# A linear attention and MLP kernel on one core: the second MLP product formed from seven sub-block products, in a new instruction order

## The chip, the cores and the metric

The kernel runs on one core of a Trainium2 chip. A core has TensorE (PE; its weight loads, PEld, overlap its matmuls), VectorE (DVE), ScalarE (ACT), GpSimd (POOL) and SyncE (SP), which only issues DMAs here. Each engine works through its own queue in order; waits between them are semaphores. The metric is the device time of one execution in microseconds, as the median of several runs. Before the change that is 877.42 us (three runs, 877.41 to 877.72).

## The reference

Two kinds of layers alternate, A B A B, over x of 2048 rows by 448 columns; float32 throughout:

```python
def _A_ref(x, wqkv, wo):
    B, S, D = x.shape
    H = 16; Dh = D // H
    ...
    q, k, v = qkv[0], qkv[1], qkv[2]
    phi = lambda t: jnp.where(t > 0, t + 1, jnp.exp(t)) + 1e-6
    pq, pk = phi(q), phi(k)
    kv = jnp.einsum("bhsd,bhse->bhde", pk, v)
    z = jnp.einsum("bhsd->bhd", pk)
    num = jnp.einsum("bhqd,bhde->bhqe", pq, kv)
    den = jnp.einsum("bhqd,bhd->bhq", pq, z)[..., None] + 1e-6
    o = num / den
    return (lambda x, *d: x.transpose(*d))(o, 0, 2, 1, 3).reshape(B, S, D) @ wo

def _B_ref(x, w1, b1, w2, b2):
    h = jnp.einsum("bsd,df->bsf", x, w1) + b1
    h = _gelu(h)
    return jnp.einsum("bsf,fd->bsd", h, w2) + b2

x = A_x
x = x + _A_ref(_layernorm(x, axis=-1), A_wqkv, A_wo)
x = x + _B_ref(_layernorm(x, axis=-1), B_w1, B_b1, B_w2, B_b2)
x = x + _A_ref(_layernorm(x, axis=-1), A_wqkv, A_wo)
x = x + _B_ref(_layernorm(x, axis=-1), B_w1, B_b1, B_w2, B_b2)
```

qkv is x @ wqkv, cut into q, k and v of 16 heads with 28 columns each. LayerNorm has no weights; the MLP's hidden width F is 1792.

## The kernel before, in words

**Tiles and precision.** The 2048 rows are 16 tiles of 128; four tiles are a block. A float32 product is made of fp32r matmuls: each operand is split into a high part (a cast to fp32r) and a low part (the difference), and three products high x high, high x low, low x high are summed in a PSUM bank. The last 64 of 448 columns are handled with both parts in one 128-row piece.

**The order.** `ORDER` (from line 15 on) is one string of tokens for each of the two A-B pairs. `run` goes through it; a token such as `gh13` calls the function `gh` with number 13, `:a`, `:d`, `:p` names an engine (or a buffer), `>` and `<` reach into the other pair. So the tokens' sequence is the order in every engine's queue and in SP's.

**Attention.** `ld` loads a tile of x, `a` takes its mean and variance (`stats`, lines 349 to 356: BN_STATS, BN_AGGREGATE, an addition, all VectorE), `ar` the power -0.5 on GpSimd, `n` the normalization on VectorE (`norm`, line 365). The tile is turned either by TensorE transposes (`T`, `ht`) or by 32x32 transposes on VectorE (`tu`) with a store to DRAM (`st`) and four loads that put the squares in place (`sp`). `xh` and `xl` split it. `K` and `Q` project, `ke` to `kl` and `qe`, `qp` form phi; `qs` stores phi(q) to DRAM. `G` sums x-transposed times phi(k) over all tiles; from it come kv, the mask and one matrix per group (`kv`, `mask`, `m`). Then each tile of phi(q) is loaded (`pl`), divided by its denominator (`pz` on GpSimd, `pd`, `pm` on VectorE), turned (`pT`, or `pu`, `ps`, `pp`), split (`qh`, `ql`), multiplied (`o`, `oc`) and added to x (`oa`).

**MLP.** `la` and `ln` are the LayerNorm again, into a buffer xm; `mT` or `mu`, `ms`, `mp` turn it, `yh` and `yl` split it into a block's XH and XL, of which there are two each (line 382). `lb` adds b2 to x on GpSimd. For each block `f` (lines 884 to 895) forms one of 14 chunks of 128 hidden units by 512 rows: 11 matmuls of 512 columns, into one of two `h` banks; `g` applies bias and gelu on ScalarE (line 900); `gh` casts it on ScalarE, `gl` takes the difference on VectorE (line 910), in rings A and B of two buffers. `y` (or its four parts `u`) adds a chunk to the block's four row tiles, which stay in the four `acc` banks:

```python
pe.matmul(o, gh[:, r], w2h[:, i, s], start=first, stop=False)   # L918
pe.matmul(o, gh[:, r], w2l[:, i, s], start=False, stop=False)   # L919
pe.matmul(o, gl[:, r], w2h[:, i, s], start=False, stop=last)    # L920
```

After the 14th chunk `ya` adds the bank to x (line 937) and `ys` stores the tile. The next block's attention tail (`pl` to `oa`) and LayerNorm run between a block's `f` and `y`.

**Weights.** `bld`, `bhi` and `blo` load and split w1 (n < 16) and w2 (n from 16 on) once, during the first attention; w1h, w1l, w1x, w2h and w2l stay in SBUF for both pairs.

Of the kernel before, what the change touches and what calls it, by code (L numbers as in the profile page):

```python
# [118 lines left out]
def linear_attn_mlp_kernel(  # L119
# [19 lines left out]
    NF = F // 128  # L139
    G = 112  # L140
    NG = D // G
    TL = D - 64
    LAYERS = 2

    consts = ctx.enter_context(tc.tile_pool(name="consts", bufs=1))
# [174 lines left out]
    def bhi(l, n, e):  # L320
        s = T[l, "bg", n]
        eng = ENG[e or "a"]
        if n >= 16:
            copy(eng, w2h[:, n - 16], s)
            return
# [656 lines left out]
```

## Time and profile before

| | |
|---|---|
| median of the runs | 877.42 us |
| profiled execution, span from first to last instruction | 875.6 us |
| instructions | 11616 |
| TensorE busy | 870.3 us |
| VectorE, ScalarE, GpSimd busy | 477.5, 344.2, 208.7 us |
| granted TensorE clock | 1.0 in all slices |
| DMA | 93.71 MB |

The profile is of one execution; its own device time is not listed beside it, its span is 875.6 us. The busy time of an engine is the union of its instructions' durations. Rows by line give a group of instructions: engine, operation, tiles out<-in with their sizes, count, busy us, mean ns of one, and the idle time ahead of them with what ended it. Timeline rows begin with start and duration in us. Rows by window give, for each engine, the busy us and the count.

### The profile page before, as it was taken

Reading aid. Unit: us, or ns where it says so; the run is one execution under the profiler, and the core shown is the slowest. Engines: PE = TensorE matmul, PEld = TensorE weight load, DVE = VectorE, ACT = ScalarE, POOL = GpSimd, SP = SyncE. Lnnn points to the kernel's source line nnn. Section 1 sums busy time; section 2 is a strip of 40 time slices with the busy share of each in tenths; the row PEclk is TensorE's granted clock in tenths of the full one; section 3 lists DMA queues with packets and bytes.
Section 4 is the critical chain, followed back from the end, with each engine's and each line's share of the span. In section 5 each row is a group of like instructions: output and inputs, shape, how many; then the busy total and the mean of one; then the engine's idle time right before and its main releaser. Section 6 shows DMA issues by size and latency. Waiting matters only on the chain.

```text
span 875.6 us, 11616 instructions
## 1 busy us (share of the span) xinstructions
PE 870.3 (99%) x4189; PEld 774.1 (88%) x4189; DVE 477.5 (55%) x974; ACT 344.2 (39%) x610; POOL 208.7 (24%) x247
## 2 busy tenths in 40 slices
PE   9999999999999999999999999999999999999998
PEld 7999998889888888888899999889898888888887
DVE  7887687758543534442379756875735616212112
ACT  6676744323223223322446555341332232223222
POOL 4555552543210020020022325240311110200000
PEclk9999999999999999999999999999999999999999
DMA  7666545543314203220347442363341251021101
GB/s 240 188 179 223 132 137 160 169 149 94 111 57 107 84 17 112 81 75 25 82 149 232 155 117 64 101 203 109 118 107 43 73 130 64 1 73 36 42 1 43
DMA packets 62762, 93.71 MB, mean 107 GB/s; under 512 B 8816, under 2 KB 57968, under 8 KB 62704
## 3 DMA queue, kind: packets, MB, share of 16 engines
q1 hardware_dynamic: 62400, 92.51, 35.1%
q8 instruction: 33, 0.54, 0.3%
q10 hardware_dynamic: 304, 0.46, 0.2%
q14 instruction: 25, 0.20, 0.1%
HBM read 55.65 MB, written 34.08 MB: 102 GB/s over the span
## 4 chain that ended last, share of the span: by engine, by line
PE 90%; issue 3%; DVE 2%; DMA 2%; ACT 1%; POOL 1%; SPq 0%; POOLq 0%; DVEq 0%; ACTq 0%
PE y L919 10%; PE y L918 10%; PE y L920 10%; PE hp L892 9%; PE hp L891 9%; PE hp L893 9%; PE hp L894 3%; PE hp L895 3%; PE psq L547 2%; PE psq L548 2%; PE psq L549 2%; PE op L827 2%; PE op L828 2%; PE op L826 2%; PE psk L547 1%
## 5 line engine op out<-in xcount | busy, mean ns | idle before, releaser
L910 DVE TENSOR_TENSOR gl<-g,gh 128x512 fp32r<-128x512 f32 x112 | 81.3, 729 | 265.1 <-ACT gh L215 265.1
L900 ACT ACTIVATE g<-hp,b1s 128x512 f32<-128x512 f32 x112 | 76.9, 688 | 258.1 <-PE hp L895 236.1
L919 PE MATMUL y<-w2l,gh 128*128 128x448 f32 x448 | 163.7, 365 | 0.0
L918 PE MATMUL y<-w2h,gh 128*128 128x448 f32 x448 | 163.6, 365 | 0.0
L920 PE MATMUL y<-w2h,gl 128*128 128x448 f32 x448 | 163.6, 365 | 0.0
L892 PE MATMUL hp<-XH,w1l 128*128 128x512 f32 x336 | 130.9, 390 | 0.0
L891 PE MATMUL hp<-XH,w1h 128*128 128x512 f32 x336 | 130.8, 389 | 0.0
L893 PE MATMUL hp<-XL,w1h 128*128 128x512 f32 x336 | 130.8, 389 | 0.0
L215 ACT CAST gh<-g 128x512 fp32r<-128x512 f32 x112 | 69.2, 621 | 137.8 <-PE y L919 131.7
L361 POOL TENSOR_TENSOR brs<-bve,mhalf 128x1 f32<-128x1 f32 x64 | 37.3, 586 | 358.7 <-DVE bve L355 325.5
L918 PEld LDWEIGHTS y<-w2h,gh 128*128 128x128 f32 x448 | 84.1, 188 | 7.4
L919 PEld LDWEIGHTS y<-w2l,gh 128*128 128x128 f32 x448 | 84.1, 188 | 7.3
L920 PEld LDWEIGHTS y<-w2h,gl 128*128 128x128 f32 x448 | 84.1, 188 | 6.6
L893 PEld LDWEIGHTS hp<-XL,w1h 128*128 128x128 f32 x336 | 63.1, 188 | 13.2
L891 PEld LDWEIGHTS hp<-XH,w1h 128*128 128x128 f32 x336 | 63.1, 188 | 12.6
L892 PEld LDWEIGHTS hp<-XH,w1l 128*128 128x128 f32 x336 | 63.1, 188 | 12.5
L757 POOL TENSOR_TENSOR pz<-pq,zb 128x448 f32<-128x448 f32 x32 | 37.3, 1170 | 50.0 <-DVE dn L762 37.1
L539 POOL TENSOR_TENSOR xnl<-x,xnh 128x384 fp32r<-128x384 f32 x32 | 32.6, 1017 | 58.4 <-ACT xnh L215 58.3
L351 DVE BATCH_NORM_STATS2 bst<-x 128x6 f32<-128x448 f32 x64 | 39.5, 617 | 7.7 <-DMA x<-in_A_x_dram 4.2
L894 PE MATMUL hp<-XH,w1x 128*128 128x512 f32 x112 | 43.6, 389 | 0.0
L895 PE MATMUL hp<-XL,w1x 128*128 128x512 f32 x112 | 43.6, 389 | 0.0
L855 POOL TENSOR_TENSOR x<-x,b2b 128x448 f32<-128x448 f32 x32 | 39.5, 1246 | 14.9 <-DVE xm L365 14.9
(174 smaller groups left out, 1569.2 us busy)
## 6 DMA issues: line engine op xcount, KB each, us to landing
x<-in_A_x_dram SPq DMA_DIRECT2D x32, 224.0 KB, 3.5
pq_d<-eq SPq DMA_DIRECT2D x32, 224.0 KB, 2.9
pq<-pq_d SPq DMA_DIRECT2D x32, 224.0 KB, 3.4
x<-x_d SPq DMA_DIRECT2D x32, 224.0 KB, 3.3
sq_a<-sq SPq DMA_DIRECT2D x13, 512.0 KB, 3.0
sp<-sq_a SPq DMA_DIRECT2D x52, 128.0 KB, 3.5
sq_q<-sq SPq DMA_DIRECT2D x12, 512.0 KB, 3.6
sp<-sq_q SPq DMA_DIRECT2D x48, 128.0 KB, 3.1
```

What stands on the lines that cost most here:

```text
L215: act.copy(out, src)
L351: dve.bn_stats(st, xs)
L891: pe.matmul(o, w1h[:, c, s], x.moving(x.hi, c), start=(c == 0), stop=False)
L892: pe.matmul(o, w1l[:, c, s], x.moving(x.hi, c), start=False, stop=False)
L893: pe.matmul(o, w1h[:, c, s], x.moving(x.lo, c), start=False, stop=False)
L894: pe.matmul(o, w1x[:, s], x.moving(x.hi, 3), start=False, stop=False)
L895: pe.matmul(o, w1x[:, s], x.moving(x.lo, 3), start=False, stop=True)
L900: act.activation(T[l, "g", n], T[l, "hp", n], AF.Gelu_apprx_tanh, bias=b1s[:, n % NF:n % NF + 1])
L910: dve.tensor_sub(lo, T[l, "g", n], f(hi))
L918: pe.matmul(o, gh[:, r], w2h[:, i, s], start=first, stop=False)
L919: pe.matmul(o, gh[:, r], w2l[:, i, s], start=False, stop=False)
L920: pe.matmul(o, gl[:, r], w2h[:, i, s], start=False, stop=last)
```

## The change

The second MLP product of a block, 512 rows x 1792 times 1792 x 448, is formed by Strassen's scheme: the gelu output is cut into a11, a12 (rows 0 to 255, hidden units 0 to 895 and 896 to 1791) and a21, a22 (rows 256 to 511), w2 likewise, and seven products of sums of them replace eight. 

- w2 is no longer kept in SBUF. `vd`, `va`, `vh`, `vl`, `vs` load its 14 row chunks, form the five sums of quarters, split all seven and store them to DRAM as `w2_d`, high and low part side by side, 448 columns in all. `cw` loads one of the seven (896 x 448 floats, as 7 chunks in 128 partitions) for each product, into a ring of three buffers, Y, which `vd` uses too.
- `g` writes its chunk into a store of 14 chunks: eight in the second pair of XH and XL, six in a new tile g6. The MLP's own input has one XH and XL instead of two.
- `cs` forms the sums of a block in place, on VectorE, one quarter (two chunks, the last one chunk) at a time; `ch` casts a quarter on ScalarE, `cl` takes the difference on VectorE, in rings A and B or E and F.
- `cp` multiplies a quarter: for each chunk and each of two row tiles a matmul of 448 columns (high part with both parts of the weights) and one of 224 (low part with the high part of the weights, added to the right half of the bank). A product fills two of the four `acc` banks.
- `cf` adds both halves of a bank into x, or subtracts them, for each place that the product goes to.
- LayerNorm: `stats` and `norm` can run on ScalarE (a sum by an accumulating pass, a squared pass, then the scaling). 28 of 32 MLP tiles and 14 of 32 attention tiles (`n` only) use that.
- `pz` stays on GpSimd in all its tokens; its default engine is now VectorE.
- Both strings of `ORDER` are new. The first wqkv pieces are all loaded by SP, and the first product is Q of tile 0 instead of K.

```diff
...
-        "gh0 bld21:xn pd5 bhi18 bhi21 gl0 f1 g1 u0 gh1 gl1 u3 u1 pz4 u2 y1 f2 pm5 pd4 f3 g2 gh2 mc g3 blo18 "
...
+        "cw1 cp4 cp5 pp3 qh6 cw2 qs13 ql6 mu4 mu5 cs12 g11 ch7 ms2 oc6 ch6 cl9 cl6 cp6 qh7 oa6 ql7 oc7 cs5 cs9 la6:a "
...
+        "ys14 ch106 ch107:aEF cl106 cl107 cf51 ys15 cp104 cp105 cp106 cp107 ch109:aEF ch108 cl108 cp108 cl109 cp109 "
+        "ch110 ch111:aEF cl110 cp110 cl111 cp111 cf53 cf52 cf54 ys12 cf55 ys13 "
...
     TL = D - 64
+    HD = D // 2
+    KC = NF // 2
     LAYERS = 2
...
-    BUFS = {"H": 9, "S": 5, "e": 3, "xn": 2, "A": 2, "B": 2, "E": 2, "F": 2, "X": 2, "tail": 2, "small": 2}
+    BUFS = {"H": 9, "S": 5, "e": 3, "xn": 2, "A": 2, "B": 2, "E": 2, "F": 2, "X": 2, "tail": 2, "small": 2, "Y": 3}
     BANKS = {"acc": 4, "h": 2, "m": 2}
...
     pq_d = [dram([S, D], F32, f"pq_d{l}") for l in range(LAYERS)]
+    w2_d = dram([7, 128, KC * D], F32, "w2_d")
     x_d = [x0] + [dram([S, D], F32, f"x_d{l}") for l in range(1, LAYERS)] + [y_out]
     make_identity(nc, ident)
+    eps = consts.tile([128, 1], F32, name="eps")
+    pool.memset(eps, 1e-5)
     mhalf = consts.tile([128, 1], F32, name="mhalf")
...
     w1x = wts.tile([128, F], F32R, name="w1x")
-    w2h = wts.tile([128, NF, D], F32R, name="w2h")
-    w2l = wts.tile([128, NF, D], F32R, name="w2l")
+    g6 = wts.tile([128, 6, 512], F32, name="g6")
...
         s = T[l, "bg", n] = ring(tag, 512 if tag == "xn" else D, "stg")[:, :D]
-        if n < 16:
-            load_piece(w1[:, n // 4 * D:(n // 4 + 1) * D], n % 4, s, sp)
-        else:
-            sp.dma_start(s, w2[rows(n - 16), :])
+        load_piece(w1[:, n // 4 * D:(n // 4 + 1) * D], n % 4, s, sp)
         eng = ENG[e or "a"]
-        if n >= 16:
-            copy(eng, w2h[:, n - 16], s)
-            return
         sl, c = slice(n // 4 * D, (n // 4 + 1) * D), n % 4
...
         eng = ENG[e or "p"]
-        if n >= 16:
-            eng.tensor_tensor(w2l[:, n - 16], s, f(w2h[:, n - 16]), op=OP.subtract)
-            return
         sl, c = slice(n // 4 * D, (n // 4 + 1) * D), n % 4
...
-    def stats(xs):
+    M3, M6, M4, M1, M2, M5, M7 = range(7)
+    W2AT = (1, 5, 2, 4, 0, 3, 6)
+    GOES = {M1: ((0, 0, OP.add), (1, 1, OP.add)), M2: ((1, 0, OP.add), (1, 1, OP.subtract)),
+            M3: ((0, 1, OP.add), (1, 1, OP.add)), M4: ((0, 0, OP.add), (1, 0, OP.add)),
+            M5: ((0, 1, OP.add), (0, 0, OP.subtract)), M6: ((1, 1, OP.add),), M7: ((0, 0, OP.add),)}
+    @op
+    def vd(l, i, e):
+        T["w2o", l, i] = o = ring("Y", KC * D, "w2o").rearrange("p (k h n) -> p k h n", k=7, h=2)
+        for r in range(2):
+            sp.dma_start(o[:, 2 * r:2 * r + 2, 1], w2[rows(r * KC + i), :].rearrange("p (h n) -> p h n", h=2))
+    @op
+    def va(l, i, e):
+        o = T["w2o", l, i][:, :, 1]
+        eng = ENG[e or "p"]
+        for to, x, y, how in ((4, 0, 3, OP.add), (5, 0, 1, OP.add), (6, 2, 3, OP.add),
+                              (1, 1, 3, OP.subtract), (2, 2, 0, OP.subtract)):
+            eng.tensor_tensor(o[:, to], o[:, x], o[:, y], op=how)
+    @op
+    def vh(l, i, e):
+        hi, lo = (T["w2o", l, i][:, :, h] for h in range(2))
+        copy(ENG[e or "a"], hi.bitcast(F32R), lo)
+    @op
+    def vl(l, i, e):
+        hi, lo = (T["w2o", l, i][:, :, h] for h in range(2))
+        (ENG[e or "p"]).tensor_tensor(lo.bitcast(F32R), lo, hi, op=OP.subtract)
+    @op
+    def vs(l, i, e):
+        sp.dma_start(w2_d[:, :, i * D:(i + 1) * D].rearrange("k p n -> p k n"),
+                     T["w2o", l, i].rearrange("p k h n -> p k (h n)"))
+    def stats(xs, e, other):
+        ve = small(1, "bve")
+        mv = small(2, "bmv")
+        if e == "a":
+            act.activation(xs, xs, AF.Identity, accum_out=mv[:, 1:2])
+            act.mul(mv[:, 0:1], mv[:, 1:2], -1.0 / D)
+            act.activation(other(), xs, AF.Square, bias=mv[:, 0:1], accum_out=mv[:, 1:2])
+            act.activation(ve, mv[:, 1:2], AF.Identity, bias=eps, scale=1.0 / D)
+            return mv, ve, True
         st = small(6, "bst")
         dve.bn_stats(st, xs)
-        mv = small(2, "bmv")
         dve.bn_aggr(mv, st)
-        ve = small(1, "bve")
         dve.tensor_scalar(ve, mv[:, 1:2], 1e-5, None, op0=OP.add)
-        return mv, ve
+        return mv, ve, False
     def root(key):
-        mv, ve = T[key]
+        mv, ve, neg = T[key]
         rs = small(1, "brs")
         pool.tensor_tensor(rs, ve, mhalf, op=OP.pow)
-        T[key] = mv, rs
-    def norm(out, xs, mv, rs):
-        dve.tensor_scalar(out, xs, mv[:, 0:1], rs, op0=OP.subtract, op1=OP.mult)
+        T[key] = mv, rs, neg
+    def norm(out, xs, mv, rs, neg, e):
+        if e == "a":
+            nb = small(1, "bnb")
+            if not neg:
+                act.mul(mv[:, 0:1], mv[:, 0:1], -1.0)
+            act.activation(nb, mv[:, 0:1], AF.Identity, scale=rs)
+            act.activation(out, xs, AF.Identity, bias=nb, scale=rs)
+        else:
+            dve.tensor_scalar(out, xs, mv[:, 0:1], rs, op0=OP.add if neg else OP.subtract, op1=OP.mult)
     class Block:
-        def __init__(self):
-            self.hi = ring("XH", 2048, "XH", F32R)
-            self.lo = ring("XL", 2048, "XL", F32R)
+        def __init__(self, r):
+            self.hi = ring(f"XH{r}", 2048, "XH", F32R)
+            self.lo = ring(f"XL{r}", 2048, "XL", F32R)
...
-    BUFS["XH"] = BUFS["XL"] = 2
-    def block(*key):
+    def block(kind, l, b):
+        key = (kind, l, b) if kind == "a" else (kind, l)
         if ("blk", key) not in T:
-            T["blk", key] = Block()
+            T["blk", key] = Block(b % 2)
         return T["blk", key]
...
     def a(l, t, e):
-        T["st", l, t] = stats(T["x", l, t])
+        T["st", l, t] = stats(T["x", l, t], e, lambda: ring("e", 512, "sj")[:, :D])
...
         xs = T["xn", l, t] = T["x", l, t]
-        norm(xs, xs, *T["st", l, t])
+        norm(xs, xs, *T["st", l, t], e)
...
     def pz(l, t, e):
-        T["pz", l, t] = ring(e or f"W{4 if t > 3 else 4 + t % 2}", D, "pz")
-        pool.tensor_tensor(T["pz", l, t], T["pq", l, t], T[l, "zb"], op=OP.mult)
+        T["pz", l, t] = ring(f"W{4 if t > 3 else 4 + t % 2}", D, "pz")
+        ENG[e or "d"].tensor_tensor(T["pz", l, t], T["pq", l, t], T[l, "zb"], op=OP.mult)
...
     def la(l, t, e):
-        T["st", l, t] = stats(T["x", l, t])
+        def xm():
+            T["mn", l, t] = ring("xn", 512, f"xm{l}_{t}")
+            return T["mn", l, t][:, :D]
+        T["st", l, t] = stats(T["x", l, t], e, xm)
     def ln(l, t, e):
-        xn = T["mn", l, t] = ring("xn", 512, f"xm{l}_{t}")
-        mv, rs = T["st", l, t]
-        norm(xn[:, :D], T["x", l, t], mv, rs)
+        if ("mn", l, t) not in T:
+            T["mn", l, t] = ring("xn", 512, f"xm{l}_{t}")
+        norm(T["mn", l, t][:, :D], T["x", l, t], *T["st", l, t], e)
     def lx(l, t, e):
-        mv, rs = T["st", l, t]
-        norm(T["mn", l, t][:, D:], T["x", l, t][:, TL:], mv, rs)
+        norm(T["mn", l, t][:, D:], T["x", l, t][:, TL:], *T["st", l, t], e)
...
+    def gstore(l):
+        if (l, "G2") not in T:
+            T[l, "G2"] = [ring(t, 2048, "g2").rearrange("p (c n) -> p c n", c=4) for t in ("XH1", "XL1")]
+        return T[l, "G2"]
+    def gview(l, half, c, k=1):
+        return gstore(l)[half][:, c:c + k] if c < 4 else g6[:, half * 3 + c - 4:half * 3 + c - 4 + k]
     @op
     def g(l, n, e):
-        T[l, "g", n] = ring("e", 512, "g")
-        act.activation(T[l, "g", n], T[l, "hp", n], AF.Gelu_apprx_tanh, bias=b1s[:, n % NF:n % NF + 1])
-    @op
-    def gh(l, n, e):
-        T[l, "gs", n] = ring("A", 512, "gh", F32R), ring("B", 512, "gl", F32R)
-        copy(ENG[e or "a"], T[l, "gs", n][0], T[l, "g", n])
-    @op
-    def gl(l, n, e):
-        hi, lo = T[l, "gs", n]
-        dve.tensor_sub(lo, T[l, "g", n], f(hi))
-    def y_mm(l, n, j, s=slice(0, D), o=None):
-        gh, gl = T[l, "gs", n]
         i = n % NF
-        first, last = i == 0, i == NF - 1
-        r = rows(j)
-        o = T[l, "y", n // NF, j][:, s] if o is None else o
-        pe.matmul(o, gh[:, r], w2h[:, i, s], start=first, stop=False)
-        pe.matmul(o, gh[:, r], w2l[:, i, s], start=False, stop=False)
-        pe.matmul(o, gl[:, r], w2h[:, i, s], start=False, stop=last)
-    @op
-    def y(l, n, e):
-        for j in range(4):
-            u(l, n * 4 + j, e)
-    @op
-    def u(l, n, e):
-        n, j = divmod(n, 4)
-        if n % NF == 0:
-            T[l, "y", n // NF, j] = bank("acc", f"y{j}")[:, :D]
-        y_mm(l, n, j)
-    @op
-    def ya(l, t, e):
-        xs = T["x", l, t]
-        dve.tensor_tensor(xs, T[l, "y", t // 4, t % 4], xs, op=OP.add)
+        act.activation(gview(l, i // KC, i % KC)[:, 0], T[l, "hp", n], AF.Gelu_apprx_tanh, bias=b1s[:, i:i + 1])
+    def quad(l, r, c, q):
+        return gview(l, c, q * 2, min(2, KC - q * 2))[:, :, r * 256:(r + 1) * 256]
+    def sums(l, n):
+        bk, q = divmod(n, 4)
+        return quad(l, *{M3: (0, 0), M4: (1, 1), M2: (1, 0), M5: (0, 1), M1: (0, 0), M6: (1, 0), M7: (1, 1)}[bk % 7], q)
+    @op
+    def cs(l, n, e):
+        s, q = n // 4 % 5, n % 4
+        a11, a12, a21, a22 = quad(l, 0, 0, q), quad(l, 0, 1, q), quad(l, 1, 0, q), quad(l, 1, 1, q)
+        to, x, y, how = ((a21, a21, a11, OP.subtract), (a12, a12, a11, OP.add), (a11, a11, a22, OP.add),
+                         (a21, a21, a11, OP.add), (a22, a12, a11, OP.subtract))[s]
+        ENG[e or "d"].tensor_tensor(to, x, y, op=how)
+    @op
+    def ch(l, n, e):
+        x = sums(l, n)
+        w = x.shape[1]
+        T[l, "chl", n] = [ring(t, 512, nm, F32R)[:, :w * 256].rearrange("p (c n) -> p c n", c=w)
+                          for t, nm in zip(e[1:] or "AB", ("ch", "cl"))]
+        copy(ENG[e[:1] or "a"], T[l, "chl", n][0], x)
+    @op
+    def cl(l, n, e):
+        hi, lo = T[l, "chl", n]
+        ENG[e or "d"].tensor_tensor(lo, sums(l, n), f(hi), op=OP.subtract)
+    @op
+    def cw(l, n, e):
+        T[l, "w2", n] = ring("Y", KC * D, "w2s", F32R).rearrange("p (c n) -> p c n", c=KC)
+        ENG[e or "s"].dma_start(f(T[l, "w2", n].rearrange("p c n -> p (c n)")), w2_d[W2AT[n % 7]])
+    @op
+    def cp(l, n, e):
+        bk, q = divmod(n, 4)
+        hi, lo = T[l, "chl", n]
+        w = T[l, "w2", bk]
+        if q == 0:
+            T[l, "cp", bk] = [bank(e or "acc", f"cp{j}")[:, :D] for j in range(2)]
+        for c in range(hi.shape[1]):
+            i = q * 2 + c
+            for j in range(2):
+                o = T[l, "cp", bk][j]
+                pe.matmul(o, hi[:, c, rows(j)], w[:, i], start=(i == 0), stop=False)
+                pe.matmul(o[:, HD:], lo[:, c, rows(j)], w[:, i, :HD], start=False, stop=(i == KC - 1))
+    @op
+    def cf(l, n, e):
+        bk, j = divmod(n, 2)
+        b, k = divmod(bk, 7)
+        o = T[l, "cp", bk][j]
+        for part in (o[:, :HD], o[:, HD:]):
+            for r, c, how in GOES[k]:
+                xs = T["x", l, 4 * b + 2 * r + j][:, c * HD:(c + 1) * HD]
+                dve.tensor_tensor(xs, xs, part, op=how)
```

More of the change, by code (lines that the diff above doesn't have):

```diff
@@ L902, in gh @@
-    @op
-    def gh(l, n, e):
-        T[l, "gs", n] = ring("A", 512, "gh", F32R), ring("B", 512, "gl", F32R)
-        copy(ENG[e or "a"], T[l, "gs", n][0], T[l, "g", n])
-    @op
-    def gl(l, n, e):
-        hi, lo = T[l, "gs", n]
-        dve.tensor_sub(lo, T[l, "g", n], f(hi))
-    def y_mm(l, n, j, s=slice(0, D), o=None):
-        gh, gl = T[l, "gs", n]
-        i = n % NF
-        first, last = i == 0, i == NF - 1
-        r = rows(j)
-        o = T[l, "y", n // NF, j][:, s] if o is None else o
-        pe.matmul(o, gh[:, r], w2h[:, i, s], start=first, stop=False)
-        pe.matmul(o, gh[:, r], w2l[:, i, s], start=False, stop=False)
-        pe.matmul(o, gl[:, r], w2h[:, i, s], start=False, stop=last)
@@ L922, in y @@
-    @op
-    def y(l, n, e):
-        for j in range(4):
-            u(l, n * 4 + j, e)
-    @op
-    def u(l, n, e):
-        n, j = divmod(n, 4)
-        if n % NF == 0:
-            T[l, "y", n // NF, j] = bank("acc", f"y{j}")[:, :D]
-        y_mm(l, n, j)
-    @op
-    def ya(l, t, e):
-        xs = T["x", l, t]
-        dve.tensor_tensor(xs, T[l, "y", t // 4, t % 4], xs, op=OP.add)
+        i = n % NF
+        act.activation(gview(l, i // KC, i % KC)[:, 0], T[l, "hp", n], AF.Gelu_apprx_tanh, bias=b1s[:, i:i + 1])
```

212 rows, old and new, of the table ORDER are left out of this document.

## The prediction

> **What bounds the kernel now.** I read the page first: busy time, slices, DMA queues, chain of the end.
>
> ```profile
> PE 870.3 (99%) x4189; PEld 774.1 (88%) x4189; DVE 477.5 (55%) x974; ACT 344.2 (39%) x610; POOL 208.7 (24%) x247
> DVE  7887687758543534442379756875735616212112
> DMA  7666545543314203220347442363341251021101
> q1 hardware_dynamic: 62400, 92.51, 35.1%
> PE 90%; issue 3%; DVE 2%; DMA 2%; ACT 1%; POOL 1%; SPq 0%; POOLq 0%; DVEq 0%; ACTq 0%
> ```
>
> TensorE is busy 870.3 of 875.6 us and is 90% of the chain that ended last. VectorE has room where the MLP runs alone (digits 1 to 4), little in the attention stages (7 to 9). The busy times by stretch show it in us; the columns are PE, PEld, DVE, ACT, POOL, clock, DMA share, GB/s:
>
> ```profile
> 50.00:100.00 50.00, 49.89 (x246) 45.92 (x245) 37.19 (x70) 34.62 (x68) 27.68 (x33) 1.00 0.61 178
> 300.00:350.00 50.00, 50.00 (x237) 43.98 (x236) 19.15 (x34) 15.32 (x25) 7.68 (x8) 1.00 0.26 82
> 750.00:800.00 50.00, 50.00 (x236) 43.97 (x235) 11.42 (x20) 15.39 (x25) 0.00 (x0) 1.00 0.14 43
> ```
>
> So time moves with what TensorE must issue, as long as the other engines feed it. A matmul's duration overlaps the next one's, so its price is the step from start to start. The timeline of TensorE in an MLP stretch:
>
> ```profile
> 829.84 0.36 PE L920 MATMUL y<-w2h,gl 128*128 128x448 f32 x1
> ...
> 832.27 0.36 PE L920 MATMUL y<-w2h,gl 128*128 128x448 f32 x1
> 832.47 0.39 PE L891 MATMUL hp<-XH,w1h 128*128 128x512 f32 x1
> ...
> 834.96 0.39 PE L891 MATMUL hp<-XH,w1h 128*128 128x512 f32 x1
> ```
>
> From 829.84 to 832.27 are 12 steps of 448 columns, 0.2025 us each; from 832.47 to 834.96 are 11 of 512, 0.2264 us each.
>
> **The change: TensorE.** A block of 512 rows had 14 chunks x 4 row tiles x 3 = 168 matmuls of 448 columns: 168 x 0.2025 = 34.0 us. Now it has 7 products x 7 chunks x 2 row tiles = 98 pairs: one matmul of 448 columns (high part of the sums against the weights' high and low parts side by side) and one of 224 (low part against high). No row shows this kernel's fp32r matmul at 224 columns. The nearest are the short ones, and the weight loads around them:
>
> ```profile
> 109.95 3.31 PE L681 MATMUL kvp<-gt,wvt 128*112 128x112 f32 x32
> 113.03 0.45 PE L547 MATMUL psq<-wq,XH 128*128 128x448 f32 x1
> 129.30 1.04 PE L394 MATMUL tp<-ident,xm 128*128 128x128 f32 x8
> 130.09 0.45 PE L547 MATMUL psq<-wq,XH 128*128 128x448 f32 x1
> 113.00 0.19 PEld L547 LDWEIGHTS psq<-wq,XH 128*128 128x128 f32 x1
> 113.11 0.19 PEld L548 LDWEIGHTS psq<-wq,XH 128*128 128x128 f32 x1
> ```
>
> The 32 short ones take (113.03 - 109.95) / 32 = 0.096 us each (kv's operands are plain float32, which gives two records a matmul), the eight transposes (130.09 - 129.30) / 8 = 0.099; one weight load follows another after 113.11 - 113.00 = 0.11. In columns a 224 step would be 0.101 (half of 0.2025); the line through the 448 and 512 steps gives 0.119; I take 0.11, the load's pitch, since every one of the 196 matmuls brings its own load. The pairs then take 98 x 0.3125 = 30.6 us a block: 3.4 saved, x 8 blocks = **27.2 us**. Ends: 0.101 gives 34.1 saved, 0.119 gives 20.1. If instead the short ones show a rate (0.096 / 112 = 0.86 ns a column), 224 columns take 0.192, a pair 0.3945, a block 38.7, and 37 us are lost: a rival below.
>
> The Trainium skill, page "TensorE: Matmul & The Clock Gate", section "LDWEIGHTS (loading the stationary operand)", says that a load takes its columns divided by 1.2 GHz, so an estimate of 107 ns for 128; the pitch of 0.11 agrees. Its section "Back-to-back issue gap" alone gives an estimate of 96 ns for 224 columns, with which the saving would be 38 us; by the load rule it is 29 us, and no run here shows a 224 step yet.
>
> **VectorE.** Its durations overlap too: the timeline groups three on one line, and the groups by line give durations.
>
> ```profile
> 119.01 1.68 DVE L727 TENSOR_TENSOR Ml<-mp,Mh 112x448 fp32r<-112x448 f32 x3
> L727 DVE TENSOR_TENSOR Ml<-mp,Mh 112x448 fp32r<-112x448 f32 x8 | 4.4, 608 | 0.0
> L910 DVE TENSOR_TENSOR gl<-g,gh 128x512 fp32r<-128x512 f32 x112 | 81.3, 729 | 265.1 <-ACT gh L215 265.1
> L937 DVE TENSOR_TENSOR x<-y,x 128x448 f32<-128x448 f32 x32 | 19.1, 617 | 10.4 <-PE y L920 10.3
> L481 DVE TENSOR_TENSOR XL<-tp,XH 128x256 fp32r<-128x256 f32 x4 | 1.6, 421 | 1.0 <-ACT XH L215 1.0
> L351 DVE BATCH_NORM_STATS2 bst<-x 128x6 f32<-128x448 f32 x64 | 39.5, 617 | 7.7 <-DMA x<-in_A_x_dram 4.2 <-DMA x<-x_d 2.9
> L365 DVE TENSOR_SCALAR xm<-x,bmv,brs 128x448 f32<-128x448 f32 x32 | 23.5, 738 | 10.6 <-POOL brs L361 10.5
> ```
>
> (1.68 - 0.608) / 2 = 0.54: a slot is the duration less some 0.08. So 512 columns cost 0.65, 256 cost 0.34, and 224, from 421 and 617 by 1.02 ns a column, 0.39 - 0.08 = 0.31. A block's products bring per product three quarters of 512 and one of 256. cl: 21 x 0.65 + 7 x 0.34 = 16.0. cs (5 sums, 4 quarters): 15 x 0.65 + 5 x 0.34 = 11.5. cf: 48 additions x 0.31 = 14.9. Together 42.4; gone are 14 gl (9.1) and 4 ya (2.2): +31.1 a block, +249 in all. LayerNorm for 28 MLP tiles leaves, 28 x (0.617 + 0.738) = 38 without the small ones; 14 attention norms leave, some 7; preparing w2 brings about 18 (20 additions of 224, seven differences of 1568). VectorE goes from 477 to about 700 us, 81% of the new span: not the sum's bound. TensorE has per block 14 x 11 x 0.2264 = 34.9 for f and 30.6 for the products, 65.5 against 42.4.
>
> By stretches it is tighter, for the next block's attention adds to it. I went through the new order and summed each engine's slots for every 30 us of TensorE work. VectorE exceeds TensorE by 11 us in all (most behind f26 and f49 of the first layer and in the last block); with stretches of 50 us by 3, with 10 us by 35. Buffers bridge a few us, not 50: two ring pairs for ch/cl, three for weights, two hp banks. I charge the 30 us figure, **+11 us**, and keep 3 and 35 as ends.
>
> **ScalarE and GpSimd.** ch replaces gh:
>
> ```profile
> L215 ACT CAST gh<-g 128x512 fp32r<-128x512 f32 x112 | 69.2, 621 | 137.8 <-PE y L919 131.7
> L237 ACT ACTIVATE spare<-mhalf 128x1 f32<-128x1 f32 x4 | 0.8, 195 | 0.0
> ```
>
> Per block 21 x 0.62 + 7 x 0.37 for 14 x 0.62 is +6.9, +55 in all. A moved LayerNorm is three passes of about 0.6 and three small ones of 0.2, 2.4 us x 28 = 67; 14 norms 13; the w2 cast 10. ScalarE reaches about 490 us, 57%: nothing, with the gaps of the MLP stages as cover. GpSimd loses 14 differences and gains three sets of sums: nothing.
>
> **DMA.** Every product loads its weights again: 128 x 7 x 448 x 4 B = 1.6 MB, 56 times, and seven stores of as much: 101 MB on top of 93. The queue's share rises from 35% to about 74%. No row shows a transfer of 1.6 MB:
>
> ```profile
> GB/s 240 188 179 223 132 137 160 169 149 94 111 57 107 84 17 112 81 75 25 82 149 232 155 117 64 101 203 109 118 107 43 73 130 64 1 73 36 42 1 43
> sq_a<-sq SPq DMA_DIRECT2D x13, 512.0 KB, 3.0
> out_dram<-x SPq DMA_DIRECT2D x16, 224.0 KB, 2.0
> ```
>
> The first slice moved 240 GB/s at share 0.7, so full share would be some 340: 4.7 us of moving, behind some 2 us as in the smallest row here: 7, and up to 11 with the queue shared. Three buffers, freed by the product's last matmul, and 9.4 us of TensorE per product (65.5 / 7) cover it at nothing. In the last five products, 4.4 us each with no f between them, cover is 8.8 us; if a load takes 11, three of them are late by 2.2 each, a rival below. The skill's "DMA: Bandwidth & Descriptors", section on one DMA's anatomy, fits 2.0 us plus bytes at 436 GB/s for another issue path: an estimate of 5.7 us, with which that rival would be nothing. Behind a weight load that waits for its buffer stand on SP's queue the next x tiles, the spreads of the turned tiles and the stores; ScalarE's yh and qh wait for the spreads. The MLP's input also has one buffer instead of two: yh of the next block waits for the last f; ten quarters of products (12 us) stand there in the new order as cover.
>
> **Both ends.** The timeline at the end:
>
> ```profile
> 870.28 2.38 DVE L937 TENSOR_TENSOR x<-y,x 128x448 f32<-128x448 f32 x4 [1.92 <-PE y L920]
> ...
> 871.63 0.37 PE L920 MATMUL y<-w2h,gl 128*128 128x448 f32 x1
> ```
>
> The last addition ends 0.66 us behind the last matmul. Now four additions of 224 follow the last pair, 4 x 0.31 + 0.3: **+0.9**. At the start Q0 needs all four pieces of wq ahead of any K, where hk0 needed two of wk; their loads come one behind another on SP instead of on two queues: **+1.5**, ends 0 and 3.
>
> **Sum.** 875.6 - 27.2 + 11 + 0.9 + 1.5 = 861.8. The median, 877.4, is 1.8 above the profiled span: **863.6 us**.
>
> **Rivals.** (a) The 224-column matmul runs at the rate of the short ones, 0.192 instead of 0.11: 784 x 0.082 = 64 more, **928 us**, slower. It decides from a step of 0.128 on, where 784 x 0.0175 eats the remaining 13.8. For it: no row shows a short fp32r one. Against: short rows and load pitch agree on 0.10 to 0.11 whatever the columns. (b) VectorE's queue can't be levelled: what it owes in stretches of 10 us comes out as waits of cp for cl: +35 for 11, **888 us**. For it: order is strict, and cs, ch, cl, cp are a chain over three engines with two buffers. Against: neighbours of the full stretches have room. (c) Weight loads come late at the end and in runs of three products: 11 instead of 7 us, 3 x 2.2 + some 5: **875 us**. (d) Nothing waits and short steps go by columns: 875.6 - 34.1 + 0.9 + 1.5 + 1.8 = **846 us**. That the products are not fewer columns is excluded by count: 98 x 672 against 168 x 448 is seven eighths.
>
> **How the numbers follow.** Chances: forecast 0.62 (its own range 849 to 873), (a) 0.10, (b) 0.10, (c) 0.08, (d) 0.10. Range 846 to 893: without (a) and the lower half of (d). About 0.2% is what a measurement of this kernel can tell. Faster: forecast, (d) and half of (c), 0.76; same: the other half, 0.04; slower: (a) and (b), 0.20.
>
> **What would show it.** Start to start 0.11 behind a 448-column cp and 0.20 behind a 224 one; TensorE's idle time about 14 us more, released by cl and by DMA into w2s; VectorE near 700 us busy. A pair over 0.33 breaks the first term; PE idle above 25 us breaks the second; weight loads of over 9 us make (c).

## The result and the profile after

The kernel with the change takes **864.06 us** (median of four runs, 863.68 to 864.35) against 877.41 for the kernel before, run beside it: a ratio of 0.9848, 95% interval 0.9834 to 0.9862, so 1.5% faster. The profiled execution took 864.35 us, 1.8 more than its span of 862.6, the same distance that the prediction had assumed for the kernel before.

The page of the changed kernel: span, busy times, VectorE's row of slices, the hardware DMA queue, the three costliest groups of the new product, and the weight loads from issue to landing.

```profile
span 862.6 us, 13265 instructions
PE 849.5 (98%) x4413; PEld 754.4 (87%) x4413; DVE 682.6 (79%) x1499; ACT 496.2 (58%) x985; POOL 209.1 (24%) x249
DVE  6977899779879867958998766747896895586588
q1 hardware_dynamic: 78944, 194.12, 67.3%
L1036 PE MATMUL cp<-w2s,ch 128*128 128x448 f32 x784 | 251.1, 373 | 1.7 <-DVE x L1048 1.7
L1037 PE MATMUL cp<-w2s,cl 128*128 128x224 f32 x784 | 208.1, 265 | 0.7 <-DVE cl L1018 0.6
L1048 DVE TENSOR_TENSOR x<-x,cp 128x224 f32<-128x224 f32 x384 | 124.4, 379 | 14.2 <-PE cp L1037 12.6
w2s<-w_d SPq DMA_DIRECT2D x56, 1568.0 KB, 7.8
```

TensorE still bounds the kernel: 849.5 of 862.6 us. Its busy time fell by 20.8 and its idle time rose from 5.3 to 13.1. VectorE went from 477.5 to 682.6 us and ScalarE from 344.2 to 496.2, as the prediction had them within 3%; in VectorE's slices the MLP's digits of 1 to 4 have become 4 to 9. The mean duration of the 224-column matmul (265 ns) is not its price, for it overlaps its neighbours. The price stands in the timeline of TensorE in the last block, where nothing but products runs:

```profile
848.87 0.38 PE L1036 MATMUL cp<-w2s,ch 128*128 128x448 f32 x1
849.08 0.26 PE L1037 MATMUL cp<-w2s,cl 128*128 128x224 f32 x1
849.18 0.38 PE L1036 MATMUL cp<-w2s,ch 128*128 128x448 f32 x1
...
853.88 0.38 PE L1036 MATMUL cp<-w2s,ch 128*128 128x448 f32 x1
...
858.20 0.26 PE L1037 MATMUL cp<-w2s,cl 128*128 128x224 f32 x1
```

From 848.87 to 853.88 are 16 pairs: 0.313 us each. The step behind the 448-column matmul is 0.21, the one behind the 224-column one 0.10.

**Where the time came from.** The first f of each pair of layers cuts the span into stages; the timeline of TensorE has it, in the kernel before

```profile
137.88 0.40 PE L891 MATMUL hp<-XH,w1h 128*128 128x512 f32 x1
...
569.04 0.39 PE L891 MATMUL hp<-XH,w1h 128*128 128x512 f32 x1
```

and in the changed one:

```profile
143.14 0.50 PE L971 MATMUL hp<-XH,w1h 128*128 128x512 f32 x1 [0.67 <-ACT XH L247]
...
564.68 0.39 PE L971 MATMUL hp<-XH,w1h 128*128 128x512 f32 x1
```

| stage | before | after | difference |
|---|---|---|---|
| start to first f (695 matmuls in both) | 137.9 | 143.1 | +5.3 |
| first f to first f of the second pair | 431.2 | 421.5 | -9.6 |
| from there to the start of the last matmul | 302.6 | 293.5 | -9.1 |
| behind it | 4.0 | 4.4 | +0.4 |
| span | 875.6 | 862.6 | -13.0 |

By steps the product saves 1344 x 0.2025 = 272.2 less 784 x 0.3135 = 245.8, so 26.4 us (0.3135 lies between this stretch and that of e1 below). The two middle rows show 18.7. So 7.7 us of that were lost in the two middle stages (both MLPs and the second attention), and 5.3 in the first attention, where the same matmuls run as before.

Less than half of the 7.7 is waiting. TensorE's windows of the two middle stages (length, busy and instructions, granted clock, DMA share, GB/s), before and after:

```profile
137.88:569.04 431.16, 431.01 (x2075) 1.00 0.36 108
569.04:871.63 302.59, 302.59 (x1420) 1.00 0.24 72
```

```profile
143.14:564.68 421.54, 420.00 (x2186) 1.00 0.69 230
564.68:858.20 293.52, 291.55 (x1532) 1.00 0.62 215
```

TensorE idles there for 1.54 + 1.97 = 3.5 us, and for 0.15 in the kernel before. The largest other part is f itself, where it stands directly behind a product:

```profile
596.03 0.40 PE L971 MATMUL hp<-XH,w1h 128*128 128x512 f32 x1
...
598.57 0.36 PE L1036 MATMUL cp<-w2s,ch 128*128 128x448 f32 x1
```

These eleven matmuls take 598.57 - 596.03 = 2.54 us, where the prediction counts 2.49: the first ten steps behind a product are a few ns longer. That happens 67 times in the two stages and comes to some 3 us in all. A little over one us remains open.

### The profile page after: what moved, and what is told of

It is laid out like the page before. It is cut to its first block, busy times and chain, and to the rows that moved or that the text cites. A ratio compares the mean times of both kernels' runs of the same rounds, so it can differ in the third digit from the quotient of the medians.

```text
span 862.6 us, 13265 instructions
## 1 busy us (share of the span) xinstructions
PE 849.5 (98%) x4413; PEld 754.4 (87%) x4413; DVE 682.6 (79%) x1499; ACT 496.2 (58%) x985; POOL 209.1 (24%) x249
## 3 DMA queue, kind: packets, MB, share of 16 engines
q1 hardware_dynamic: 78944, 194.12, 67.3%
## 4 chain that ended last, share of the span: by engine, by line
PE 87%; DVE 4%; ACT 3%; DMA 2%; SPq 1%; issue 1%; POOL 0%; DVEq 0%; ACTq 0%; POOLq 0%
PE cp L1036 18%; PE cp L1037 9%; PE hp L971 9%; PE hp L973 9%; PE hp L972 9%; PE hp L974 3%; PE hp L975 3%; PE G L700 2%; PE G L699 2%; PE G L698 2%; PE op L903 2%; PE psk L624 2%; PE op L905 2%; PE op L904 2%; PE psk L626 2%; PE psk L625 2%
## 5 line engine op out<-in xcount | busy, mean ns | idle before, releaser
L1036 PE MATMUL cp<-w2s,ch 128*128 128x448 f32 x784 | 251.1, 373 | 1.7 <-DVE x L1048 1.7
L1037 PE MATMUL cp<-w2s,cl 128*128 128x224 f32 x784 | 208.1, 265 | 0.7 <-DVE cl L1018 0.6
L247 ACT CAST ch<-g 128x512 fp32r<-128x512 f32 (+1 forms) x224 | 123.5, 565 | 127.2 <-PE cp L1036 103.4
L1018 DVE TENSOR_TENSOR cl<-g,ch 128x512 fp32r<-128x512 f32 (+1 forms) x224 | 139.5, 642 | 63.8 <-ACT ch L247 63.0
L1036 PEld LDWEIGHTS cp<-w2s,ch 128*128 128x128 f32 x784 | 147.1, 188 | 14.8 <-issue 2.2
L1037 PEld LDWEIGHTS cp<-w2s,cl 128*128 128x128 f32 x784 | 149.4, 191 | 5.2 <-DVE cl L1018 2.3
L1048 DVE TENSOR_TENSOR x<-x,cp 128x224 f32<-128x224 f32 x384 | 124.4, 379 | 14.2 <-PE cp L1037 12.6
L1005 DVE TENSOR_TENSOR g<-g 128x512 f32<-128x512 f32 (+1 forms) x112 | 66.8, 609 | 9.4 <-ACT g L988 8.7
L834 POOL TENSOR_TENSOR pz<-pq,zb 128x448 f32<-128x448 f32 x32 | 40.8, 1276 | 130.6 <-DMA pq<-pq_d 81.4
L509 DVE TENSOR_TENSOR XL<-sp,XH 128x512 fp32r<-128x512 f32 x50 | 35.6, 734 | 2.6 <-ACT XH L247 2.5
```

The source lines that it names most:

```text
L247: act.copy(out, src)
L1005: ENG[e or "d"].tensor_tensor(to, x, y, op=how)
L1018: ENG[e or "d"].tensor_tensor(lo, sums(l, n), f(hi), op=OP.subtract)
L1036: pe.matmul(o, hi[:, c, rows(j)], w[:, i], start=(i == 0), stop=False)
L1037: pe.matmul(o[:, HD:], lo[:, c, rows(j)], w[:, i, :HD], start=False, stop=(i == KC - 1))
L1048: dve.tensor_tensor(xs, xs, part, op=how)
```

## The experiments

All ratios are to the kernel before, measured beside each.

**e1: what prices the short matmul.** The second matmul of a pair with half its columns:

```diff
-                pe.matmul(o[:, HD:], lo[:, c, rows(j)], w[:, i, :HD], start=False, stop=(i == KC - 1))
+                pe.matmul(o[:, HD:HD + 112], lo[:, c, rows(j)], w[:, i, :112], start=False, stop=(i == KC - 1))
```

> The short matmul of a pair (L1037) takes 112 columns instead of 224; half of the low-part product is left out. The profile of the changed kernel has a pair of 448 and 224 columns at 0.313 us. Theory (the step behind a short matmul is set by its neighbour's weight load, about 0.11): a pair stays at 0.31, the time stays within 4 us of 864. Rival (the step goes by columns, 0.42 ns each, plus a fixed 0.016): a pair takes 0.266, 784 pairs save 37 us, the time is 828 if nothing else takes over.

Measured 865.83 us (two runs), ratio 0.987 (0.9851 to 0.989). Half the columns give no time at all. The timeline of e1, TensorE and then its weight loads:

```profile
849.83 0.42 PE L1036 MATMUL cp<-w2s,ch 128*128 128x448 f32 x1
850.09 0.21 PE L1037 MATMUL cp<-w2s,cl 128*128 128x112 f32 x1
850.14 0.42 PE L1036 MATMUL cp<-w2s,ch 128*128 128x448 f32 x1
...
852.34 0.42 PE L1036 MATMUL cp<-w2s,ch 128*128 128x448 f32 x1
```

```profile
849.78 0.19 PEld L1036 LDWEIGHTS cp<-w2s,ch 128*128 128x128 f32 x1
849.89 0.19 PEld L1037 LDWEIGHTS cp<-w2s,cl 128*128 128x128 f32 x1
850.10 0.19 PEld L1036 LDWEIGHTS cp<-w2s,ch 128*128 128x128 f32 x1
```

Eight pairs in 2.51 us are again 0.314 each, although the start-to-start steps are now 0.26 and 0.05. The weight loads start 0.11 and 0.21 apart, the rhythm of the changed kernel. A matmul of 224 columns therefore isn't paid by its columns: one of 112 costs the same. This settles rival (a): there is no rate of 0.86 ns a column. That the floor of some 0.10 us is the weight load fits this rhythm, but isn't shown: every short matmul in these traces brings a load of its own, and no run has one without, so a fixed price of any short matmul would look the same.

**e3 and e10: what VectorE's new work costs.** e3 adds 16 of each half's 224 columns into x; e10 narrows the in-place sums too. Both leave out part of the computation.

```diff
-                dve.tensor_tensor(xs, xs, part, op=how)
+                dve.tensor_tensor(xs, xs, part[:, :16], op=how)
```

(with xs cut to the same 16 columns), and in e10 also

```diff
-        ENG[e or "d"].tensor_tensor(to, x, y, op=how)
+        ENG[e or "d"].tensor_tensor(to[:, :, :16], x[:, :, :16], y[:, :, :16], op=how)
```

> cf adds 16 of each 224 columns into x; the other columns of the additions are left out, all waits stay. VectorE loses about 384 x 0.2 = 80 us. Theory (what TensorE waits for in the MLP stages is VectorE's load): the 5 us or so of waits there go, the time falls by 4 to 7 us, to 857 to 860; the waits of the first 150 us stay. Rival (those waits are the order's and the chains' latencies, not VectorE's load): the time falls by less than 2 us.

> The changed kernel with both the additions into x (cf) and the in-place sums (cs) on 16 columns of a chunk or half instead of all, so some 170 us less of VectorE in the MLP stages. Theory: what VectorE costs in the changed kernel are the few waits of TensorE there, about 6 us in the two MLP stages, of which e3 took 4; so 858 to 860, and no more than 2 us below e3. Rival: the sums hold up the whole chain (cs, ch, cl, cp) and with them go the stretches that I charged 11 us for: 853 or less.

Measured: e3 860.23 us, ratio 0.9807 (0.9792 to 0.9821); e10 860.90, 0.9817 (0.9799 to 0.9835). VectorE's busy time fell to 609.6 and 543.5 us, but beyond e3 nothing more came: 139 us less of VectorE are worth 3 to 4 us, all of it from the additions into x. The changed kernel shows the place, in TensorE's waits (us in total, times, longest) and in the chain of work ahead of the longest one:

```profile
PE cp L1036 <- DVE x L1048: 1.7, 2, 0.8
```

```profile
697.66 0.94 ACT ch L247 x2
698.62 0.69 DVE cl L1018
699.33 1.04 DVE x L1048 x4
...
700.53 0.68 DVE cl L1018
701.21 0.82 DVE x L1048 x3
...
702.64 0.44 PE cp L1036
```

A new product needs two banks, and its first matmul waits until VectorE has gone through cl, cf, cl, cf, one behind another. TensorE stands from 701.54 + 0.26 to 702.64. This happens twice, at 701.5 and 777.6. Without the additions both waits are gone; 139 us less of VectorE still leave the two middle stages 4.6 us longer than the steps alone would (712.0 against 733.8 - 26.4). Hardly any of that remainder is waiting: TensorE idles in these stages of e10 for 1.2 us only (420.22 - 419.14 and 291.79 - 291.65), and the f behind a product are as long as in the changed kernel, 2.9 us in all.

**e4, e12: why the first attention is longer.** e4 leaves out the four tokens that load activation tables early (two at the start, two in the middle of the first attention). e12 keeps them and issues two of the first four wq loads on ScalarE's queue.

```diff
-        "fl ld1 a1 ar1 hot16 tab0 tab1 ld0 ...
+        "fl ld1 a1 ar1 hot16 ld0 ...
```

(and `>tab0`, `>tab1` likewise); e12:

```diff
-        "fl ld1 a1 ar1 hot16 tab0 tab1 ld0 a0 ar0 n1 n0 wqld2 wqh2 d1 ht3 ht2 wqld0 wqh0 wql0 wqld1 ...
+        "fl ld1 a1 ar1 hot16 wqld0:a wqld3:a tab0 tab1 ld0 a0 ar0 n1 n0 wqld2 wqld1 wqh2 d1 ht3 ht2 wqh0 wql0 ...
```

> The tokens tab0 and tab1 at the start and in the middle of the first attention are taken out, so that ScalarE's activation tables are loaded only where a function needs them: five loads of 1.28 us fewer by the trace, 1 to 3 added. Theory (the gelu table loaded at the start costs a reload ahead of the first exp, on the path at 17 us, and again near 81 us): the time falls by 1 to 2.5 us, to 861.6 to 863. Rival (TensorE's queue has work that hides them): within 0.5 us of 864.1.

> The changed kernel with two of the four first wq loads issued on ScalarE's queue, as the kernel before did with wk. If the loads on one queue cost the 1.5 us that the prediction charged for the start, 862.2 to 863. If the start is late for another reason (the table loads, that e4 took away), 863.5 to 864.7.

Measured: e4 863.09 us, ratio 0.9839 (0.9823 to 0.9854); e12 864.29, 0.9855 (0.9835 to 0.9875). The queue of the loads gives no gain. The tables cost something at the place itself: in the changed kernel the chain of work at the start runs through a table load between the two passes that form phi,

```profile
16.39 0.55 ACT ek L634
...
16.96 1.28 ACT L635
...
18.25 0.59 ACT ek L635
18.86 0.63 DVE psk L639
```

and the groups by line count eight of them instead of four: three by the tokens themselves, three for exp at L635 (before: one) and two for gelu (before: two, and one at a cast):

```profile
L269 ACT ACT_TABLE_LOAD x3 | 3.8, 1283 | 0.8 <-PEq L1081 0.8
L635 ACT ACT_TABLE_LOAD x3 | 3.8, 1283 | 0.1
L988 ACT ACT_TABLE_LOAD x2 | 2.6, 1283 | 0.0
```

A table loaded early for gelu pushes out that of exp, which is then loaded again; in e4 no load stands between the two passes (15.79 and 16.37). By the start times of TensorE's matmuls, the 160th comes at 35.0 us in the kernel before, at 38.1 in the changed one and at 36.3 in e4; the first f of e4 comes at 141.49 instead of 143.14. One pair of traces can't carry these 1.65 us, for the start scatters: nine traces with the changed kernel's order up to there (its own and those of e1, e2, e3, e5, e8, e9, e10, e13) have their first f between 142.09 and 144.25, at the mean 143.2. The two that only leave out the tokens there, e4 and e6, have it at 141.49 and 141.79, below all nine; so some 1.5 us are likely. The median keeps 1.0 of them, and the intervals of the two ratios overlap: a gain of the whole isn't shown. In this one pair of traces e4's first attention is still 3.6 us longer than that of the kernel before: 1.3 are there by matmul 160, 1.0 more by matmul 500 and 1.3 more in the output stage behind it.

**e5: the LayerNorm of the MLP back on VectorE.** The order stays as it is.

```diff
-... la4:a oc5 ... la5:a ch2 cl2 cl3 ln4:a ...
+... la4 oc5 ... la5 ch2 cl2 cl3 ln4 ...
```

> The changed kernel with the LayerNorm of the 28 MLP tiles back on VectorE (la and ln; the order of all instructions is kept). About 28 x 2 passes x 0.55 = 31 us go to VectorE, whose additions into x were worth about 4 us when 111 us of them were taken away (e3). Theory A, VectorE is short only in places: busy 682 becomes about 715 and the time rises by 1 to 4 us, 865 to 868, most of it in the MLP stages, where la and ln stand between cl and cf. Rival B, VectorE has no slack left where these tiles are normalized: every us of it is late, +15 to +30, 880 or more. Rival C, LayerNorm on ScalarE makes no difference: 864.

Measured 885.07 us, ratio 1.0083 (1.0066 to 1.01): slower than the kernel before. VectorE's busy time rises by 38 us only, the time by 21. The time is that of this expectation's rival B, and VectorE's slack is lopsided: 139 us less give 3, 38 us more cost 21. The page and TensorE's waits of e5:

```profile
PE 859.2 (97%) x4413; PEld 758.9 (86%) x4413; DVE 720.7 (82%) x1611; ACT 418.9 (47%) x761; POOL 214.0 (24%) x249
```

```profile
PE cp L1039 <- DVE cl L1020: 8.5, 11, 1.9
PE tp L471 <- DVE xm L443: 5.4, 2, 2.8
```

TensorE's idle time rises from 13.1 to 24.5 us, and its busy time by another 9.7, though it runs the same 4413 matmuls; about half of that (5.1 us) is a slower clock, shown at the end, so the 21 are not all waits for VectorE. What this run can't tell is what an order made for LayerNorm on VectorE would give, for here la and ln stand where they were put for ScalarE. LayerNorm on ScalarE alone, in the kernel before, wasn't tried.

**e2, e8, e9, e13: are the weight loads hidden?** Behind every cw, e2 copies half as much again from DRAM to DRAM on SyncE's queue, 45 MB in all; e9 the same on ScalarE's queue; e8 copies 4 KB on SyncE's queue; e13 leaves out every other load, and with it part of the computation.

```diff
+        sp.dma_start(dram([128, KC * D // 2], F32, f"more{l}_{n}"), w2_d[W2AT[n % 7]][:, :KC * D // 2])    # e2; e9: act.
+        sp.dma_start(dram([1, 1024], F32, f"more{l}_{n}"), w2_d[W2AT[n % 7]][:1, :1024])                    # e8
+        if (l, "w2", n ^ 1) in T:                                                                           # e13, ahead of the load
+            T[l, "w2", n] = T[l, "w2", n ^ 1]
+            return
```

> Each of the 56 weight loads is followed on SP by a copy of half its size from DRAM to DRAM that nobody reads: 45 MB more to move. Theory (weight loads are hidden: nothing on TensorE waits for one, and three buffers cover 9 us): within 3 us of 864. Rival (part of the 13 us that the change did not gain is weights that come late): each load lands some 2 us later, the time grows by 10 us or more.

> The changed kernel with a copy of 4 KB behind every weight load, on SyncE's queue, where e2 had one of 0.8 MB. If e2's 18 us came from the 56 more issues on SyncE's queue, this costs 10 to 18 us too (874 to 882); if they came from the bytes, it costs under 2 us (863 to 866).

> The changed kernel with e2's copies of 0.8 MB, issued on ScalarE's queue instead of SyncE's. If the bytes on the DMA engines cost e2's 18 us, this gives 875 to 890. If it was that loads stood behind the copies on SyncE's queue, this gives 864 to 870 (56 issues on ScalarE, which is busy 58% of the time).

> The changed kernel with a weight load for every other product only; the one behind it uses the same weights, so 28 loads of 1.6 MB and 45 MB are left out (and with them part of the computation). If the loads are hidden, as the prediction had it, this gives 863 to 864.5. If they contend with the other transfers even now, 862 or less, and TensorE's waits for ch, XH and tails go down.

Measured: e2 882.16 us, ratio 1.006 (1.0041 to 1.0078); e8 864.00, 0.9848 (0.9833 to 0.9863); e9 888.84, 1.0137 (1.0089 to 1.0185); e13 863.32, 0.9843 (0.9825 to 0.9861). Half of the loads less gives nothing that can be told apart, 56 more issues give nothing, and 45 MB more cost 18 us on SyncE's queue and 25 on ScalarE's, where the four runs spread from 884.78 to 895.18. So the loads are hidden as the kernel stands, and it is bytes, not issues, that stop being hidden. My theory for e2 (within 3 us) was wrong; its rival had the size, but not the reason, for the loads land after 8.4 us at the median instead of 7.8. TensorE's waits in e2 say how:

```profile
PE cp L1038 <- DVE cl L1018: 4.0, 7, 1.9
PE hp L971 <- ACT g L988: 3.3, 3, 1.5
PE cp L1037 <- DMA w2s<-w_d: 1.9, 2, 1.5
```

Only 1.9 us are waits for weights (4.9 in e9). The rest are waits for VectorE and ScalarE. Ahead of three of the four longest, the chain of work goes back to a long transfer: 9.0 us for a tile of phi(q) ahead of the wait that ends at 298.5, 9.8 and 9.1 us for a tile of x ahead of those that end at 377.1 and 759.6 (in the changed kernel the medians are 4.1 and 3.2). The queue's share rose only from 67.3% to 78.2%.

**e6, e11: can the waits be ordered away?** Both start from e4. e6 moves three groups in the second pair: cf19 with cf20, cf33 with cf34, cl100 ahead of cs75. e11 moves in addition five sums of the second pair behind them, and ml2 ahead of pd3 in the first pair.

```diff
-... cp43 cf18 ch44 yh8 cl44 cf20 ch46 ... cs37 cf19 ...
+... cp43 cf18 ch44 yh8 cl44 cf19 ch46 ... cs37 cf20 ...        # e6
-... cs26 cs30 cs34 cl38 ... cs27 cs31 cs35 cl39 ...
+... cs26 cs30 cl38 ... cs27 cs31 cl39 ... cs34 ch46 ... cs35 ch47:aEF ...   # e11; cs52, cs54, cs55 likewise
```

> The changed kernel without the four early table loads (as e4) and with three instruction groups moved in the second pair: cf19 and cf33 each change places with the cf behind them, so that a new product finds both banks of the product before the last one free, and cl100 goes ahead of cs75. Theory: the three waits of about 1.0, 1.0 and 0.5 us of TensorE for cp go and nothing follows, 860.5 to 861.5. Rival: the wait comes back at the next product, since VectorE has as much to do as before: 862.5 to 863.5, as e4.

> e6 with the sums that only the next product but one needs (cs34, cs35, cs52, cs54, cs55 of the second pair) moved behind the cl and cf that TensorE waits for, and ml2 ahead of pd3 in the first pair. Theory: VectorE is short only for some us at these places, and the two waits of 0.75 us for a bank and about 1 us ahead of the first o go: 859 to 860.5. Rival: VectorE owes as much a few us later, so the waits move to the next product: 861.3 to 862.3 as e6.

Measured: e6 861.81 us (861.39 to 862.53), ratio 0.9823 (0.9809 to 0.9838), the fastest of the versions that compute everything; against the changed kernel's 0.9848 the intervals still overlap, so its 2 us are not settled. It didn't come as I had thought: the two waits for a bank only went from 1.7 to 1.5 us together, because cf19 now stands exactly where cf20 stood in VectorE's queue. e11 takes 867.04 us, 0.9887 (0.987 to 0.9904), slower than e6 by 5, against my expectation. The move of ml2 did what it should, by half of what I had expected: from matmul 500 to the first f e11 takes 34.4 us, where the twelve other traces of the new order all take 34.9 to 35.0. (Its first f comes at 140.89 instead of e6's 141.79, but part of that is the start's scatter.) The sums, moved out of the way of cl, were now late for ch, which waits 3.2 us for one of them, and TensorE waits for both (timeline of e11):

```profile
777.25 0.47 PE L1033 MATMUL cp<-w2s,ch 128*128 128x448 f32 x1 [0.48 <-ACT ch L244]
777.98 0.37 PE L1034 MATMUL cp<-w2s,cl 128*128 128x224 f32 x1 [0.26 <-DVE cl L1015]
779.26 0.71 PE L1033 MATMUL cp<-w2s,ch 128*128 128x448 f32 x1 [0.91 <-DVE x L1045]
```

In all three orders TensorE waits here for VectorE, directly or through ch; that no order avoids it isn't shown.

## Why the prediction was right, and where it wasn't

The time (863.6 forecast, 864.06 measured) is right, and the first term carries it. Two other terms were wrong in opposite directions and nearly cancelled, 3.3 us too much and 3.8 too little; that the total came within 0.5 us is luck.

- **TensorE's steps, -27.2.** Right in size, and the columns don't set the short step, as e1 shows. A pair was put at 0.3125 and takes 0.3135, which gives -26.4. The reason given, the load's pitch, fits, but no run separates it from a fixed price of a short matmul. In "what would show it" I had the two steps the wrong way round: 0.21 lies behind the 448-column matmul and 0.10 behind the short one. The 0.11 and 0.20 are the rhythm of the loads.
- **VectorE, +11.** The mechanism is right (short stretches in which cl and cf stand behind each other), the size is not: taking most of the new work away gives 3 to 4 us, near the lower end that I had kept. The count by stretches of 30 us was too pessimistic, since VectorE can run ahead in the stretch before. Its total was predicted as 700 and is 682.6. Nor were the places the predicted ones; the two longest waits lie in the middle of the second MLP. In all, the two middle stages gave back 7.7 us. About 3 of them are the longer f behind a product, which the prediction had at nothing: it priced f and the pairs each by a stretch of its own kind. So 11 against 7.7 is nearer than the term deserves.
- **Start, +1.5.** Too small, and the cause was wrong. The first attention takes 5.3 us more (4.2 to 6.4 over the nine traces). e12 shows no gain from a second queue for the loads; e4 and e6 make it likely that some 1.5 us come from early table loads, which the prediction didn't look at. It had counted ScalarE's work and not which function tables the new order swaps. The rest is spread over the whole stage. The preparation of w2 runs there too, but no run took it away, so its share stays open.
- **DMA, nothing.** Right: e13. Loads land after 7.8 us at the median against the 7 that was worked out, and the queue's share is 67.3% for 74%. How near the edge this stands I had not seen: 45 MB more cost 18 to 25 us.
- **ScalarE and GpSimd, nothing.** Right for the casts and LayerNorm: 496.2 us against the forecast 490, and TensorE's waits that ScalarE ended come to 2.5 us. The table loads are the exception.
- **The end, +0.9.** By the start of the last matmul +0.4. The last addition ends 1.26 us behind it (858.20 + 0.26 to 858.19 + 1.53), 0.6 more than before.
- **Rivals.** (a) falls with e1, (c) with e13 (no wait of TensorE in the changed kernel is released by a weight load). (b), which ends slower too, did not happen, but e5 shows that it was not far: with 38 us more on VectorE the time is 885, near the 888 that the rival gave, though 5 us of it are the clock's, which the rival didn't have. So the move of LayerNorm to ScalarE isn't a side matter; in this order it is what lets the seven products pay. (d) failed at both halves: TensorE waits, and the pair doesn't go by columns.

## What to carry to other kernels

A matmul that brings its own weights had a floor of some 0.10 us here, so cutting one of 224 columns to 112 bought nothing. By the same figures two of 112 would cost two floors and one of 224 costs one, so merging should pay below 224 columns (an estimate; no run did it). Before adding work to an engine that is 55% busy, look for the few us where its work stands in a row: relief elsewhere gives little (139 us less gave 3 here), and more work can cost over half of its own time (38 us more cost 21). Waits moved by reordering tend to come back at the next consumer, so run each such move by itself.

## What the hardware showed that I had not expected

**TensorE's clock is cut by how long it stood still in a window of 3.41 us, not by the length of a wait.** In e5 TensorE stops for 1.87 us, from 276.90 to 278.77, and at 279.92 its clock falls to half for 3.41 us. All the changes of the clock inside e5, which lie at 279.92, 283.33, 566.64, 570.05, 576.88 and 580.29, are whole multiples of 3.41 us apart, and so are those inside e9. So I laid windows on that grid (length, PE busy and instructions, granted clock, DMA share, GB/s). In e5:

```profile
276.51:279.92 3.41, 1.54 (x10) 1.00 0.19 73
279.92:283.33 3.41, 3.41 (x13) 0.50 0.65 223
358.43:361.85 3.42, 1.88 (x12) 1.00 0.56 220
```

In e11, and in e2, whose grid I set by the fall of its clock behind the last matmul:

```profile
775.78:779.19 3.41, 1.82 (x9) 1.00 1.00 320
779.19:782.61 3.42, 3.35 (x11) 0.50 1.01 433
```

```profile
373.18:376.59 3.41, 2.00 (x9) 1.00 0.00 1
376.59:380.00 3.41, 2.92 (x18) 1.00 0.95 295
```

e2's wait of 1.91 us (375.18 to 377.08) lies across the border of two windows, with 1.41 and 0.49 us of idle time in them, and leaves the clock at 1.00; so does one of 2.07 us in e9. e11's three waits of 0.48, 0.26 and 0.91 us put 1.58 us into one window, and the clock falls. Over all 14 traces, between the first 15 us and the last matmul, seven windows at full clock had 1.58 us or more of idle time, and the clock was half in the next one each time; none with 1.54 or less did that. Where the grid lies differs from trace to trace, so the same wait may cost nothing or some 1.7 us (half of 3.41).

At half clock a pair takes some 0.59 instead of 0.31 us. e5's mean clock is 0.994, about 5 of its 21 us. In e9's profiled execution, the slowest of its four (895.18 us), it is 0.989, about 10 of 31 us. The single waits of 0.8 us in the changed kernel left the clock at 1.00. The Trainium skill, page "TensorE: Matmul & The Clock Gate", part 1 on the clock gate, gives half rate until about 3.4 us of sustained work have passed, and the trace agrees with its 3.4. It puts the loss behind an idle window of about 3.4 us; here a window with 1.58 us of standstill sufficed, and the measurement decides.

**An activation table load took 1.283 us** wherever it stood, before and after the change: more than twice a pass over 448 columns (0.55 to 0.59), so one that lands between two passes of a chain is felt.
